# Attention and a gated feed-forward block in one kernel: output groups split in halves of 192 columns, single steps paired, value halves moved behind output steps

## The chip, the cores and the metric

The kernel runs on one core of a Trainium2 chip. A core has five engines with a queue each: TensorE (PE) for matrix products, VectorE (DVE) and ScalarE (ACT) for elementwise work, GpSimd (POOL), and SyncE (SP), which issues transfers. TensorE writes to PSUM, eight banks of 512 float32 columns by 128 partitions; everything else lies in SBUF. An engine works off its instructions in the order in which they were written; between engines, semaphores hold an instruction back until what it reads is there, or until the buffer that it overwrites has been read. The metric is the device time of one execution in microseconds.

## The reference

Eight batches of twelve heads, 448 positions, 64 columns a head; then a feed-forward block over 3584 tokens of 768 columns, with 1536 hidden columns. All inputs are float32, and the kernel loads them as float16.

```python
scores = np.matmul(q, k.transpose(0, 1, 3, 2)) / np.sqrt(64)
attn = np.exp(scores - np.max(scores, -1, keepdims=True))
attn = attn / (np.sum(attn, -1, keepdims=True) + 1e-09)
x = np.matmul(attn, v).transpose(0, 2, 1, 3).reshape(3584, 768)
g = x @ w_gate
out = (g / (1 + np.exp(-g)) * (x @ w_val)) @ w_out
```

## The kernel before

**Attention.** Heads go in 48 pairs. `qk` makes the scores of one chunk of keys for the two heads of a pair, transposed (keys on partitions, 2 x 448 queries in columns), in a tile `s` of two banks; ACT takes the exponential into `E` (L366 for the later pairs). `pv` multiplies `E` with the values, to which a column of ones is attached, into two accumulators `acc` (one bank each); DVE divides by the sums (L480, L481) into `xt`, and a transposing DMA on SP's queue puts that into `X`, with the 768 columns on partitions and tokens in columns. POOL's queue loads q, k and v and POOL copies q and k (L238) for the next pairs.

**Feed-forward, first half.** Tokens go in blocks of 384 and 512 columns. A `Step` makes one block of 128 hidden columns: a gate product `gp` (six matmuls, L586), ACT's tanh `sg` (L613), DVE's `t` = (sg + 1) gp (L639), a value product `vp`, and DVE's `hts` = t vp (L645). A block has twelve steps. `run_pair` runs two steps interleaved: the gate of one, the gate of two, the value of one, then the value of two *split* in halves of columns. The first half goes into a bank that step one left free (`spare`, shown as gp in the rows of the value weights), the second into a bank of its own (vp). `run_single` runs one step alone, split in the same way; `run_fv` runs one whole.

**Feed-forward, second half.** `OutPair.wide` makes the output of two chunks of 128 tokens, called a *group* below, with seven products in place of eight, from sums that DVE makes beforehand (`h_sums`, L569 to L572; the sums of the weights stay in SBUF). Each product is six matmuls of 128 x 384 (`OH` = 384), and they share three banks, a, c (both in tile `og`) and b (tile `ob`):

| product | bank | then |
|---|---|---|
| P1 | a | ACT copies it to p1 (L765) |
| P2 | c | DVE makes p15 from it and p1 (L767) |
| P3 | b | DVE writes p15 and b back to c (L760) |
| P4 | a, added to P1 | ACT copies it to the output (L772) |
| P5 | b, over P3 | DVE makes an output quarter of b and p15 (L760) |
| P6 | c, added to what DVE wrote | ACT copies it to the output (L783) |
| P7 | b, added to P5 | DVE makes the last quarter with p1 (L760) |

So P4 can't start before the copy to p1 has read a, and neither P5 nor P7 before DVE has read b. A third chunk of a block of 384 is done plainly, in four *output steps* of 12 matmuls of 192 columns (`plain_out`, L679), which ACT copies out (L686). Outputs collect in `osb` (four buffers) and are stored through SP's queue (L669).

**Order.** Pairs of heads and feed-forward are interleaved by hand in *visits*, one for each entry of a list. A visit issues, in this order: the scores of three chunks with their exponentials, the accumulations `pv` of one pair of heads, and then feed-forward work. One visit in seven has no accumulations; it is called bare. From the visit `base` on, which is visit 0 here, the list `VISITS` says what the work is: `(begins, nf, ng, no, ns)`, where nf counts steps (2 is a pair, 1 a single), ng groups, no output steps, and ns extra sums. If the next visit is bare, steps run one after the other and whole. The queues of ACT and DVE get their instructions in the same order, so that a group's ACT copies stand behind the three exponentials of its visit. Tiles `s`, `gp` of a step, `og` and `op` of an output step share three buffers of two banks (`ps_s`); `acc`, `vp` and `ob` share two buffers of one bank (`ps_f`).

The visits that differ, with the time at which their scores start in the profile before:

| visit | starts | before | after |
|---|---|---|---|
| 11 | 189.05 | group | half group |
| 12 | 197.51 | output step | pair, last half put off |
| 13 | 200.30 | pair | output step, put-off half |
| 14 | 207.23 | output step | output step, half group |
| 15 | 209.89 | pair | pair, last half put off |
| 16 | 216.99 | output step | output step, put-off half |
| 17 (bare) | 219.61 | pair | pair, last half put off |
| 18 | 225.82 | output step | output step, put-off half |
| 22 | 246.62 | group | half group |
| 23 | 255.08 | single (whole) | two whole steps |
| 25 | 263.50 | single | half group |
| 26 | 267.27 | group | pair |
| 27 | 276.12 | single | half group |
| 29 | 285.79 | single | half group |

Visits 19 to 21, 24 and 28 are pairs, 30 and 31 output steps, in both kernels; visits 0 to 10 are the same. After visit 31 come the last blocks, in `Unit`s (products with seven matmul chains of their own, L855) and groups, which the change leaves alone; POOL makes weight sums for them (L818 to L821) from visit 26 on.

Of the kernel before, what the change touches and what calls it, by code (L numbers as in the profile page):

```python
# [10 lines left out]
FP32 = mybir.dt.float32  # L11
FP16 = mybir.dt.float16
AF = mybir.ActivationFunctionType
# [3 lines left out]
HS = 4096.0  # L17
# [48 lines left out]
def kernel(  # L66
# [10 lines left out]
    nc = tc.nc  # L77
# [636 lines left out]
    class OutPair:  # L714
# [26 lines left out]
        def stored(self, z, lo=0, w=DM, queues=(nc.sync,)):  # L741
            store(self.osb[z], self.kk, self.c0 + (2 * self.t + z) * 128, 128, lo, w, queues, self.last)

        def wide(self, keep, add_sum, ns=(1, 2, 1)):
            osb = self.open()
            g = ps_s.tile([128, 2, 512], FP32, tag="s", name="og")
            a, c = g[:, 0, 0:OH], g[:, 1, 0:OH]
            if self.last:
                bs = ps_s.tile([128, 2, 512], FP32, tag="s", name="ob")
                parts = [(i * QW, QW, bs[:, i, 0:QW]) for i in range(2)]  # L750
            else:
                parts = [(0, OH, ps_f.tile([128, 512], FP32, tag="f", name="ob")[:, 0:OH])]
            p1, p15 = (k[:, 0:OH] for k in keep)
            both = (nc.sync, nc.scalar)

            def products(lhs, m, first=False):
                return [(lo, w, b, product(b, lhs, self.tt(m, lo, w), first)) for lo, w, b in parts]

            def combine(dst, x, scale, y, lo, w):
                return nc.vector.scalar_tensor_tensor(  # L760
                    dst[:, ds(lo, w)], x[:, ds(lo, w)] if scale == HS else x, scale, y, ALU.mult, ALU.add
                )

            product(a, self.hh(0, self.x), self.bb(0, 0, 0, OH), True)
            keep1 = nc.scalar.activation(p1, a, AF.Copy, scale=1.0 / HS)  # L765
            apart(product(c, self.hh(0, self.y), self.tt(0, 0, OH), True), keep1)
            done = [nc.vector.scalar_tensor_tensor(p15, c, 1.0 / HS, p1, ALU.mult, ALU.add)]  # L767
# [3 lines left out]
            apart(product(a, self.hh(1, self.x), self.bb(0, 1, 0, OH)), *done)  # L771
            left = nc.scalar.activation(osb[0][:, 0:OH], a, AF.Copy, scale=1.0 / HS)  # L772
            for one in done[1:]:
                tc.declare_no_dep(left.ins, one.ins, reason="another bank")
            if self.last:
                self.stored(0, 0, OH, both)
            for lo, w, b, mms in products(self.hs(1), 2):
                combine(osb[1][:, OH:], b, 1.0 / HS, p15[:, ds(lo, w)], lo, w)
            if self.last:
                self.stored(1, OH, OH, both)  # L780
            add_sum(ns[1])
            apart(product(c, self.hs(2), self.bb(1, 1, 0, OH)), left)
            nc.scalar.activation(osb[0][:, OH:], c, AF.Copy, scale=1.0 / HS)  # L783
            if self.last:
                self.stored(0, OH, OH, both)
            else:
                self.stored(0)
            ends = []
            for lo, w, b in parts:
                mms = product(b, self.hh(1, self.y), self.tt(3, lo, w))  # L790
                apart(mms, *ends)
                ends.append(combine(osb[1], b, 1.0 / HS, p1[:, ds(lo, w)], lo, w))
                if self.last:
                    self.stored(1, lo, w, both)
            if not self.last:
                self.stored(1)
            add_sum(ns[2])

# [145 lines left out]
    with tc.manual_schedule():  # L944
# [50 lines left out]
        def add_block(i, visits):  # L995
            if i < B - NB - 1:
                f1, own, n = block(i)
                fvq.extend(f1)
                kk, c0, hts = own
            else:  # L1000
                own = None
            t_out = NFB * OH / 2400.0
            if i == 0:
                oq.extend([(ffn2_steps(*own, by_half(range(n // 128), OH)), t_out)] * (2 * (n // 128)))
            if i < 2:
                if i:
# [12 lines left out]
            for pair in new:  # L1019
                pair.todo = pair.sums()  # L1020
                sums.extend(pair.todo)

        FIRST_STEPS = [2, 2, 1, 2, 1, 1, 1]
        VISITS = [
# [7 lines left out]
        ]  # L1032

# [36 lines left out]
                add_sum()  # L1070
            return 2 * step.time

        def run_pair():
            one, two = fvq.pop(0), fvq.pop(0)
            two.split, two.alone = True, gate_small[0]
            one.gate()
# [17 lines left out]
            step.finish()  # L1094
            add_sum()

        def run_steps(n):
            for _ in range(n - 2):
                run_fv()
            if n > 1:  # L1100
                run_pair()
            elif n:
                run_single()

# [105 lines left out]
        for x, (chunks, todo) in enumerate(plan):  # L1210
# [70 lines left out]
            else:  # L1281
# [177 lines left out]
```

## Time and profile before

| | |
|---|---|
| median of 3 runs | 426.39 us (426.32 to 426.64) |
| the profiled execution | 426.09 us, of which 424.3 us from first to last instruction |
| granted TensorE clock | 0.999 |
| TensorE | 4382 matmuls |
| visits 11 to 31 | 189.05 to 297.70 us |
| visit 11 (group) | 8.46 us, ACT busy 3.90, DVE 3.43 |
| visit 12 (output step) | 2.79 us, ACT busy 2.36, DVE 1.94 |
| visit 25 (single) | 3.77 us, ACT busy 2.98, DVE 2.35 |

A row of the timeline gives the start in us, the length, the engine (PEld is TensorE's weight load, which runs beside its matmuls), the line of the kernel, the operation, the tile written and those read, the shape, and how many instructions the row merges; in brackets stands how long the engine was idle before it, and for whom it waited. Matmuls overlap: one is shown some 170 ns longer than the next one's start allows, so the distance of starts is what a matmul costs.

### The profile page before, as it was taken

The page shows a single profiled execution, that of the slowest core. Times are in us where ns is not written, and L with a number is a line of the kernel's source. Part 1 is how long each engine was busy: PE and PEld are TensorE (multiplying, and loading weights), DVE is VectorE, ACT ScalarE, POOL GpSimd, SP SyncE. Part 2 cuts the span into 40 slices and gives each one's busy share as a digit, 9 for nine tenths or more (in the row PEclk, how much of TensorE's full clock was granted, in tenths as well). Part 3 has the DMA queues.
Part 4 walks back from the last instruction along what each step waited for, and adds up shares of the span by engine and source line. Part 5 has one row for each costly group of instructions (what it writes and reads, how often), then busy time and mean ns, then how long its engine had stood idle before and what let it go on. Part 6 is the DMA issues. An engine that isn't in the chain of part 4 may idle for free.

```text
span 424.3 us, 11026 instructions
## 1 busy us (share of the span) xinstructions
PE 417.6 (98%) x4382; PEld 263.7 (62%) x4382; DVE 265.2 (63%) x606; ACT 243.5 (57%) x385; POOL 229.6 (54%) x351
## 2 busy tenths in 40 slices
PE   8999999999999999999999999999999999999996
PEld 3666666655556676656656766667888655555554
DVE  4766562787669564674645765487776665565563
ACT  6976667646755654655666547569655125555221
POOL 8656625988886738349376772885999000000000
PEclk9999999999999999999999999999999999999999
DMA  9999999999999799969999999942100240000125
GB/s 137 181 201 200 200 173 192 139 159 207 135 153 152 118 147 138 170 93 177 120 130 131 133 137 149 103 115 43 22 2 19 96 122 28 2 0 2 37 76 150
DMA packets 107764, 49.73 MB, mean 117 GB/s; under 512 B 59840, under 2 KB 104512, under 8 KB 107712
## 3 DMA queue, kind: packets, MB, share of 16 engines
q0 software_dynamic: 46800, 24.56, 52.1%
q1 hardware_dynamic: 60640, 24.22, 32.6%
q8 instruction: 34, 0.56, 0.6%
q14 instruction: 18, 0.15, 0.2%
q10 hardware_dynamic: 272, 0.25, 0.2%
HBM read 49.55 MB, written 11.01 MB: 143 GB/s over the span
## 4 chain that ended last, share of the span: by engine, by line
PE 93%; ACT 3%; DVE 2%; DMA 1%; issue 1%; SPq 0%; DVEq 0%; ACTq 0%
PE gp L586 18%; PE vp L586 12%; PE un L855 10%; PE og L703 10%; PE acc L438 8%; PE ub L855 8%; PE ob L703 8%; PE s L346 5%; PE op L679 4%; PE acc L402 2%; PE s L376 2%; ACT E L384 1%; PE s L358 1%; ACT E L366 1%; PE tp L317 1%; PE op L1049 1%
## 5 line engine op out<-in xcount | busy, mean ns | idle before, releaser
L366 ACT ACTIVATE E<-s 128x896 f16<-128x896 f32 x126 | 106.6, 919 | 50.3 <-PE s L346 35.1
L238 POOL COPY qk<-qkraw 128x512 f16<-128x512 f16 x70 | 42.8, 655 | 57.3 <-DMA qkT<-qk 56.0
L586 PE MATMUL gp<-X,wg 128*128 128x384 f16 (+1 forms) x360 | 73.1, 348 | 0.0
L586 PE MATMUL vp<-X,wv 128*128 128x384 f16 (+3 forms) x360 | 64.2, 314 | 0.1
L639 DVE SCALAR_TENSOR_TENSOR t<-sg,gp 128x384 f32<-128x384 f32 (+1 forms) x60 | 36.1, 608 | 41.4 <-ACT sg L613 41.1
L586 PEld LDWEIGHTS <-wv 128*128 128x128 f16 x492 | 46.1, 98 | 24.5 <-issue 0.4
L178 POOL DMA_DIRECT2D vraw<-in_v_dram x72 | 44.1, 638 | 13.1 <-DVE hts L645 8.8
L586 PEld LDWEIGHTS <-wg 128*128 128x128 f16 x360 | 32.7, 98 | 27.2 <-issue 2.2
L178 POOL DMA_DIRECT2D qkraw<-in_k_dram x70 | 42.6, 627 | 5.8 <-DMA wo<-in_moe_w_out_dram 3.7
L384 ACT ACTIVATE E<-s 112x896 f16<-112x896 f32 x48 | 40.6, 917 | 8.0 <-PE s L376 8.0
L438 PEld LDWEIGHTS <-E 128*128 128x128 f16 (+2 forms) x1224 | 38.2, 98 | 9.2 <-issue 3.2
L613 ACT ACTIVATE sg<-gp 128x384 f32<-128x384 f32 (+1 forms) x60 | 32.0, 538 | 19.3 <-PE gp L586 16.6
L438 PE MATMUL acc<-vo,E 128*128 128x65 f16 (+2 forms) x1224 | 42.4, 193 | 0.1
L703 PEld LDWEIGHTS <-hts 128*128 128x128 f16 x270 | 25.9, 98 | 15.9
L645 DVE SCALAR_TENSOR_TENSOR hts<-t,vp 128x384 f16<-128x384 f32 (+3 forms) x60 | 31.4, 523 | 5.6 <-PE vp L586 2.1
L481 DVE TENSOR_TENSOR xt<-acc,R 128x256 f16<-128x256 f32 x72 | 30.6, 425 | 2.5
L201 POOL DMA_DIRECT2D qkraw<-in_q_dram x43 | 29.4, 685 | 4.2 <-DMA vraw<-in_v_dram 1.5
L346 PE MATMUL s<-qkT 64*64 64x448 f16 (+1 forms) x288 | 29.2, 353 | 0.5 <-DVE hts L645 0.2
L703 PE MATMUL og<-wo,hts 128*128 128x384 f16 x132 | 25.1, 326 | 0.0
L480 DVE RECIPROCAL R<-acc 128x4 f32<-128x4 f32 x72 | 12.7, 177 | 17.7 <-PE acc L438 17.5
L219 DVE COPY vo<-vraw 128x512 f16<-128x512 f16 (+1 forms) x48 | 19.7, 413 | 3.4 <-DMA vraw<-in_v_dram 3.4
L679 PE MATMUL op<-wo,hts 128*128 128x192 f16 (+1 forms) x168 | 21.4, 281 | 0.0
(185 smaller groups left out, 684.3 us busy)
## 6 DMA issues: line engine op xcount, KB each, us to landing
vraw<-in_v_dram POOLq DMA_DIRECT2D x72, 64.0 KB, 5.0
qkraw<-in_q_dram POOLq DMA_DIRECT2D x39, 112.0 KB, 4.4
qkraw<-in_k_dram POOLq DMA_DIRECT2D x68, 64.0 KB, 4.9
wg<-in_moe_w_gate_dram POOLq DMA_DIRECT2D x8, 288.0 KB, 9.8
wv<-in_moe_w_val_dram POOLq DMA_DIRECT2D x8, 288.0 KB, 10.5
wo<-in_moe_w_out_dram POOLq DMA_DIRECT2D x2, 1152.0 KB, 18.7
out_dram<-osb SPq DMA_DIRECT2D x7, 288.0 KB, 4.3
out_dram<-osb SPq DMA_DIRECT2D x6, 336.0 KB, 4.2
```

The costliest lines, as they stand in the source:

```text
L178: eng.dma_start(dst[ts(s, 64)], rows)
L238: nc.gpsimd.tensor_copy(dst.rearrange("p c h d -> p h c d"), src)
L346: nc.tensor.matmul(s[ts(half, m), hx, 0:S], lhsT=t[ts(hx, 64), ds((c + low(pr, hx)) * 128 + half * m, m)], rhs=t[ts(hx, 64), ds(NC * 128, S)],
L366: nc.scalar.activation(e[:, 0 : 2 * S].rearrange("p (h q) -> p h q", h=2), s[:, :, 0:S], AF.Exp, scale=sm_scale)
L384: nc.scalar.activation(e[:, :, 0:S], s[0:P, :, 0:S], AF.Exp, scale=sm_scale)
L438: nc.tensor.matmul(acc[ds(lo, m), ts(j, D + 1)], lhsT=e[rows, ds(hx * S + j * 128 + lo, m)], rhs=Vts[pr % NV][rows, hx, col, 0 : D + 1], s ...
L586: nc.tensor.matmul(dst[:, 0:w], lhsT=wslice(kind, self.fb, cb), rhs=X[kk][:, cb, ds(c0 + lo, w)], start=(cb == 0), stop=(cb == NCB - 1),)
L613: self.readers = [nc.scalar.activation(self.sg[:, 0:n], gp[:, 0:n], AF.Tanh, scale=0.5)]
L639: nc.vector.scalar_tensor_tensor(self.t1[:, 0:n], self.sg[:, 0:n], 1.0, self.gp[:, 0:n], ALU.add, ALU.mult)
L679: nc.tensor.matmul(op[:, 0:w], lhsT=hts[:, fb, ts(ch, 128)], rhs=wo[oh][:, fb, ds(off, w)], start=fb == 0, stop=fb == NFB - 1,)
L703: nc.tensor.matmul(dst, lhsT=lhs(n), rhs=rhs(n), start=first and n == 0, stop=n == NH - 1, skip_group_check=True)
L855: mm = nc.tensor.matmul(dst, lhsT=lhs[:, n], rhs=rhs[:, n], start=first and n == 0, stop=n == NK - 1, skip_group_check=True,)
```

## The change

`wide` takes a first column `m0` and a width `n`. With n = 192 it makes the seven products for columns m0 to m0 + 191 of both halves of the output; two calls make a group, the second one stores it. The groups of visits 2 and 6 stay whole; the three later ones are made in six halves, in visits of their own. `run_group` first runs the visit's output steps, if it has any. The single steps become members of pairs or, before the bare visit 24, whole steps. A pair that is followed by a visit with nothing but an output step leaves its last value half, six matmuls of 256 columns and DVE's product, for the end of that visit.

```diff
-        def wide(self, keep, add_sum, ns=(1, 2, 1)):
+        def wide(self, keep, add_sum, ns=(1, 2, 1), m0=0, n=OH):
...
-            a, c = g[:, 0, 0:OH], g[:, 1, 0:OH]
+            a, c = g[:, 0, 0:n], g[:, 1, 0:n]
+            at, whole = [ds(oh * OH + m0, n) for oh in range(2)], m0 + n == OH
...
-            product(a, self.hh(0, self.x), self.bb(0, 0, 0, OH), True)
+            product(a, self.hh(0, self.x), self.bb(0, 0, m0, n), True)
...
-            else:
+            elif whole:
                 self.stored(0)
...
-            (0, 2, 0, 0, 1), (0, 0, 1, 0, 0), (0, 0, 0, 1, 0), (0, 2, 0, 0, 0), (0, 0, 0, 1, 0),
+            (0, 2, 0, 0, 1), (0, 0, 1, 0, 0), (0, 2, 0, 0, 0), (0, 0, 0, 1, 0), (0, 0, 1, 1, 0),
             (0, 2, 0, 0, 0), (0, 0, 0, 1, 0), (0, 2, 0, 0, 0), (0, 0, 0, 1, 0), (0, 2, 0, 0, 0),
-            (4, 2, 0, 0, 1), (0, 2, 0, 0, 1), (0, 0, 1, 0, 0), (0, 1, 0, 0, 0), (0, 2, 0, 0, 0),
-            (0, 1, 0, 0, 0), (0, 0, 1, 0, 0), (0, 1, 0, 0, 0), (0, 2, 0, 0, 0), (0, 1, 0, 0, 0),
+            (4, 2, 0, 0, 1), (0, 2, 0, 0, 1), (0, 0, 1, 0, 0), (0, 2, 0, 0, 0), (0, 2, 0, 0, 0),
+            (0, 0, 1, 0, 0), (0, 2, 0, 0, 0), (0, 0, 1, 0, 0), (0, 2, 0, 0, 0), (0, 0, 1, 0, 0),
...
+        put_off = []
+
-        def run_pair():
+        def run_pair(later=False):
...
             two.value(0)
-            two.finish()
+            if later:
+                put_off.append(two.finish)
+            else:
+                two.finish()
...
-        def run_group():
-            pair = groups.pop(0)
+        def run_group(n):
+            pair = groups[0]
...
-            pair.wide(keep, add_sum, (1, 1, 0))
+            pair.wide(keep, add_sum, (1, 1, 0) if n == OH else (0, 1, 0), pair.begun, n)
+            pair.begun += n
+            if pair.begun == OH:
+                groups.pop(0)
...
-                for _ in range(ng):
-                    run_group()
+                if ng:
+                    for _ in range(no):
+                        run_o()
+                    run_group(ng * QW)
+                    no = 0
...
-                    run_steps(nf)
+                    run_steps(nf, nf == 2 and VISITS[x + 1 - base][1:4] == (0, 0, 1))
...
+                while put_off and not nf:
+                    put_off.pop(0)()
```

In `VISITS` the first two groups' ng becomes 2 (two quarters of 192, a whole group), so that ng now counts units of 192 columns.

More of the change, by code (lines that the diff above doesn't have):

```diff
@@ L751, in wide @@
             else:
-                parts = [(0, OH, ps_f.tile([128, 512], FP32, tag="f", name="ob")[:, 0:OH])]
-            p1, p15 = (k[:, 0:OH] for k in keep)
+                parts = [(0, n, ps_f.tile([128, 512], FP32, tag="f", name="ob")[:, 0:n])]
+            p1, p15 = (k[:, 0:n] for k in keep)
             both = (nc.sync, nc.scalar)
             def products(lhs, m, first=False):
-                return [(lo, w, b, product(b, lhs, self.tt(m, lo, w), first)) for lo, w, b in parts]
+                return [(lo, w, b, product(b, lhs, self.tt(m, m0 + lo, w), first)) for lo, w, b in parts]
             def combine(dst, x, scale, y, lo, w):
@@ L770, in wide @@
             add_sum(ns[0])
-            apart(product(a, self.hh(1, self.x), self.bb(0, 1, 0, OH)), *done)
-            left = nc.scalar.activation(osb[0][:, 0:OH], a, AF.Copy, scale=1.0 / HS)
+            apart(product(a, self.hh(1, self.x), self.bb(0, 1, m0, n)), *done)
+            left = nc.scalar.activation(osb[0][:, at[0]], a, AF.Copy, scale=1.0 / HS)
             for one in done[1:]:
@@ L777, in wide @@
             for lo, w, b, mms in products(self.hs(1), 2):
-                combine(osb[1][:, OH:], b, 1.0 / HS, p15[:, ds(lo, w)], lo, w)
+                combine(osb[1][:, at[1]], b, 1.0 / HS, p15[:, ds(lo, w)], lo, w)
             if self.last:
@@ L789, in wide @@
             for lo, w, b in parts:
-                mms = product(b, self.hh(1, self.y), self.tt(3, lo, w))
+                mms = product(b, self.hh(1, self.y), self.tt(3, m0 + lo, w))
                 apart(mms, *ends)
[L792 to L795, printed above, removed]
+                ends.append(combine(osb[1][:, at[0]], b, 1.0 / HS, p1[:, ds(lo, w)], lo, w))
+            if self.last:
+                self.stored(1, 0, OH, both)
+            elif whole:
                 self.stored(1)
@@ L1019, in add_block @@
             for pair in new:
-                pair.todo = pair.sums()
+                pair.todo, pair.begun = pair.sums(), 0
                 sums.extend(pair.todo)
@@ L1095, in run_single, with run_steps @@
             add_sum()
-        def run_steps(n):
+        def run_steps(n, later=False):
             for _ in range(n - 2):
@@ L1100, in run_steps @@
             if n > 1:
-                run_pair()
+                run_pair(later)
             elif n:
```

6 lines of the change are left out of this document (3 added, 3 removed), and 4 rows, old and new, of the table VISITS.

## The prediction

> Visits are numbered as the table above numbers them, and the seven products of a group P1 to P7 as they are issued.
>
> **What bounds the kernel now.** First the page: the share of busy time, and the chain that ended last.
>
> ```profile
> PE 417.6 (98%) x4382; PEld 263.7 (62%) x4382; DVE 265.2 (63%) x606; ACT 243.5 (57%) x385; POOL 229.6 (54%) x351
> PEclk9999999999999999999999999999999999999999
> PE 93%; ACT 3%; DVE 2%; DMA 1%; issue 1%; SPq 0%; DVEq 0%; ACTq 0%
> ```
>
> TensorE is the bound from end to end at the full granted clock, so an edit is worth what it changes on TensorE: the matmuls in its stream, and the holes between them. The stream's pitch is the same everywhere: the chain merges twelve 384-column matmuls to 1.95 us (162.5 ns each) and twelve 192-column ones to 0.99 us (82.5 ns). Both are columns / 2.4 plus 2.5 ns, with a weight load (98 ns) hidden under each. Half the columns therefore cost half the time plus 2.5 ns.
>
> Second, the holes, from the timeline of visit 11, a whole group. (The length of a PE row is modelled and runs past the next row's start; starts are what to read.)
>
> ```profile
> 189.05 0.74 PE L346 MATMUL s<-qkT 64*128 64x448 f16 x6
> 189.45 2.54 ACT L366 ACTIVATE E<-s 128x896 f16<-128x896 f32 x3 [2.31 <-PE s L346]
> 190.59 1.14 PE L703 MATMUL og<-wo,hts 128*128 128x384 f16 x6
> 191.86 0.51 ACT L765 ACTIVATE p<-og 128x384 f32<-128x384 f32 x1
> 192.81 0.56 DVE L767 SCALAR_TENSOR_TENSOR p<-og,p 128x384 f32<-128x384 f32 x1 [1.20 <-PE og L703]
> 193.51 1.14 PE L703 MATMUL og<-wo,hts 128*128 128x384 f16 x6
> 193.72 0.56 DVE L760 SCALAR_TENSOR_TENSOR og<-p,ob 128x384 f32<-128x384 f32 x1 [0.35 <-PE ob L703]
> 194.49 1.14 PE L703 MATMUL ob<-E,hsum 128*128 128x384 f16 x6
> ```
>
> The group starts at 190.59, while the three exponentials still occupy ACT to 191.99. The copy of P1 stands behind them and starts 1.27 us into the group. P4 (193.51) adds to the bank that this copy reads, P5 (194.49) overwrites the bank that the DVE combination of 193.72 reads. Both reads end before their matmul is due (192.37; 194.28): the whole group has no hole, because a product lasts 0.975 us.
>
> Third, the visits with little TensorE work: the timeline around the output step of visit 14, then the scores that follow the single steps of visits 25, 27 and 29.
>
> ```profile
> 206.03 0.69 DVE L645 SCALAR_TENSOR_TENSOR hts<-t,vp 128x512 f16<-128x512 f32 x1
> 206.49 0.82 PE L586 MATMUL vp<-X,wv 128*128 128x256 f16 x6
> 206.69 0.42 DVE L645 SCALAR_TENSOR_TENSOR hts<-t,gp 128x256 f16<-128x256 f32 x1
> 207.45 0.55 PE L346 MATMUL s<-qkT 64*64 64x448 f16 x8
> 208.81 1.15 PE L679 MATMUL op<-wo,hts 128*128 128x192 f16 x12
> 209.89 1.01 PE L346 MATMUL s<-qkT 64*128 64x448 f16 x6
> ...
> 267.49 0.85 PE L346 MATMUL s<-qkT 64*64 64x448 f16 x8
> ...
> 280.06 0.85 PE L346 MATMUL s<-qkT 64*64 64x448 f16 x8
> ...
> 289.39 0.55 PE L346 MATMUL s<-qkT 64*128 64x448 f16 x4
> 290.14 0.37 PE L346 MATMUL s<-qkT 64*128 64x448 f16 x2 [0.20 <-DVE hts L645]
> ```
>
> The score matmuls after such a visit take longer than in an ordinary one: 1.01 against 0.74 us after the output step of visit 14 (a bank waits for the exponential), 0.85 against 0.55 after the singles of visits 25 and 27, and 290.14 instead of 289.78 after the one of visit 29 (a bank waits for the last DVE product of the single). These holes are what the change can win.
>
> **The change part by part.** (1) *Holes removed.* After output steps: visit 13 0.10 (0.85 against 0.74), visit 15 0.25, visit 17 0.21 (0.15 before its second scores, 0.06 within them and behind them), visit 19 0.18. With 0.66 us of value product behind the output step, these visits last longer than three exponentials. After singles, which are gone: visits 26 and 28 0.27 each, visit 30 0.38, of which I give back 0.10 since the output step of visit 30 then comes earlier and visit 31 waits for its exponentials. After a whole group the second accumulator waits for the last 0.56 us combination: 0.09, 0.11, 0.11 in visits 12, 23, 27; with 192 columns (0.36 us) it no longer does. Sum: 0.74 + 0.82 + 0.30 = **-1.86 us**.
>
> (2) *Matmuls.* Three groups of 42 become six halves of 42, +126; four single steps (12 + 3 x 18 matmuls) become two whole steps and a pair (24 + 30), -12. 114 x 2.5 ns = **+0.29 us**.
>
> (3) *The half group's own chain.* A product is now 0.495 us. What it must cover is as long as before in its fixed parts. Durations at 192 columns: ACT copy 0.35 (output copy, L686, behind an exponential), DVE combination 0.36 (L760 at 192 columns in the last group: 0.361, 0.364); a DVE operation starts 0.03 after its releaser, a matmul 0.05; an evacuation starts 0.20 after the last matmul of its product gives way. From the start of the half: copy 1.27 to 1.62; P4 at 1.67 instead of 1.485 (hole 0.19); first DVE operation 1.66 to 2.01, combination 2.05 to 2.41; P5 at 2.455, where P4 ended at 2.17 (hole 0.285); P5 to 2.95, its combination 3.15 to 3.505; P6 to 3.445; P7 at 3.555 (hole 0.11). Together 0.58 us each in visits 11, 22, 27 and 29. Visit 25 follows a bare visit and its scores wait 0.11 themselves, so its exponentials end earlier against the group (copy at 1.10): 0.40. In visit 14 an output step (0.99) goes first, so the exponentials and that step's own copy are done 0.7 us into the group; the copy of P1 ends at 1.03, and only the two waits for DVE remain: 0.22. Sum 4 x 0.58 + 0.40 + 0.22 = **+2.94 us**. Bounds: nothing, as in the whole groups; or 0.9 each (5.4) if a DVE sum (0.55, L571) stands between the links.
>
> (4) *Value halves put off* (visits 12, 15, 17). The pair then ends with the half that goes into the first step's spare bank. Its DVE product can't start before the whole value's product ends (206.72), so it ends at 207.11 whatever TensorE does, while TensorE arrives 0.66 us sooner: the third scores of the next visit, due at 206.97, get that bank at 207.16. 0.19 us x 3 = **+0.57 us**. Below nothing is excluded, since the matmuls stay the same; above, the bound is 0.66 each. DVE's copy of v queues behind the put-off product, but it is for two visits later.
>
> (5) *Visit 23* is followed by a bare visit and so runs two whole steps; three h sums (0.55 each) stand on DVE among their four products. The second step's t then ends near 4.57 us after the visit's accumulations, its bank is wanted at 4.40 by the third scores: **+0.22 us** (0 to 0.5).
>
> (6) *At nothing:* SP's stores of two groups go out one to three visits later; SP is not the bound, four output buffers are used in the same rotation, and a store lands in about 4.3 us, far from its buffer's next use (over 20 us). POOL's loads, copies and weight sums keep their places among the visits; the sums are needed only after visit 31, which moves with them. If that cover went, POOL's 0.91 us pieces would show as holes in the units; today these are 0.08 at most.
>
> Sum: 2.94 + 0.57 + 0.22 + 0.29 - 1.86 = +2.16 us. The profiled execution took 426.09 us (span 424.3 and 1.8 around), so **428.2 us**; the median of the runs shown is 0.3 above that execution, within the spread that I leave.
>
> On the price of a narrow matmul the row says 82.5 ns at 192 columns. The Trainium skill, "TensorE: Matmul & The Clock Gate", section "Back-to-back issue gap", says that in a stream of weight loads and matmuls both set the spacing, and gives about 81 ns at 128 and 131 ns at 512 columns. An estimate between its two figures is 89 ns at 192 and 114 ns at 384, so that 252 narrow instead of 126 wide matmuls would cost 8.1 us more instead of 0.3, and the sum would be 436.0. The trace has 216 ns at 512 and 162.5 at 384 columns, so the row is used.
>
> **The rivals.** *The halves' chain is covered.* If the three waits in (3) were met in time, the change would save 1.86 and cost 1.08: 425.3 us, faster. It decides once a half waits less than 0.14 us on average (0.78 us over six). For it speaks that no whole group has a hole. Against it, the last group of all: there the first product into ob is followed by a P4 of 0.975 us and P5 still came 38 ns late, behind a 0.36 combination (417.12 to 417.17); halves have half that cover.
>
> *ACT is further ahead.* If the copy of P1 came as early in all halves as in visit 14, six halves would wait 0.22 each: 1.32 instead of 2.94, 426.6 us, no change. Against it: the exponentials start 0.40 us after a visit's first scores in every ordinary visit, and the group 1.54 after them.
>
> *DVE stands in the way.* A sum or a copy of v between the links adds 0.3 us a half: 430.0 us. For it: DVE's token sum took 1.26 us once beside POOL's sums (281.09). Against it: in program order these stand behind the chain.
>
> *The clock drops.* Waits inside a group could let the clock gate close. The granted clock was 0.999 with holes of 0.2 to 0.4 us in the rows above. At half rate six halves alone would need 3.4 us more each, 449 us. The Trainium skill's same page, section "A second HAM failure mode: psum-queue depth-cycling", tells of a kernel whose small idles between matmul groups did this; no run here shows it.
>
> **How the numbers follow.** Forecast 0.72 (427.4 to 429.2: visits 25 and 23 and the put-off waits each at their bounds). Covered 0.09, ACT ahead 0.09, DVE in the way 0.08, clock or spacing 0.02. The range reaches from the second rival, 426.4, to the third, 429.8; what lies outside is the first, the last and half of the third, 0.15. About 0.2% (0.85 us) is what a measurement tells from no change: faster 0.09, within 0.10, slower 0.81.
>
> **What would show it.** In the profile after: inside a half group P4, P5 and P7 start 0.19, 0.28 and 0.11 us after TensorE is free; ACT's copy (L766) starts 1.27 us into the half; after visits 12, 15 and 17 the scores' row grows by 0.19; the rows of 1.01 and 0.85 us are gone. The prediction is wrong if the halves show products 0.495 us apart with no hole, or if the score rows stay long.

## The result, and the profile after

The changed kernel takes 429.47 us (median of 6 runs, 429.09 to 429.71), the kernel before 426.46 on the same chip (6 runs, 426.29 to 427.11). The ratio is 1.0067, with a 95% interval of 1.0057 to 1.0077: 2.4 to 3.3 us slower. The forecast of 428.2 said slower by 2.2; the time lies inside its range of 426.4 to 429.8, but 1.3 us above the number itself and 0.3 above the inner band of 427.4 to 429.2. The profiled execution of the changed kernel took 429.71 us, with a span of 427.8.

The page of the changed kernel, its busy times, its clock and its chain:

```profile
PE 419.3 (98%) x4496; PEld 271.6 (63%) x4496; DVE 264.4 (62%) x616; ACT 245.3 (57%) x394; POOL 230.3 (54%) x351
PEclk9999999999999999999999999999999999999999
PE 90%; DVE 3%; DMA 2%; POOL 2%; ACT 2%; issue 1%; DVEq 0%; ACTq 0%; POOLq 0%
```

TensorE has the 114 matmuls more that the diff gives it (4496 for 4382), still at the full clock, and is on the chain for 90% of the span instead of 93%. Most of that difference isn't the loss: the shares of POOL and DMA lie in the first 20 us, where the chain runs through the loading of q, k and v, with 3.9 us of TensorE instead of 11.0. Within the visits, from 11 to 31, it goes through DVE for 6.3 us instead of 2.8, which points to waits. They are found by following TensorE through the visits. The timeline of visit 11, the first half group:

```profile
191.72 0.66 PE L703 MATMUL og<-wo,hts 128*128 128x192 f16 x6
192.71 0.66 PE L703 MATMUL ob<-E,hsum 128*128 128x192 f16 x6
193.00 0.35 ACT L766 ACTIVATE p<-og 128x192 f32<-128x192 f32 x1
193.38 0.36 DVE L768 SCALAR_TENSOR_TENSOR p<-og,p 128x192 f32<-128x192 f32 x1 [0.63 <-PE ob L703]
193.40 0.66 PE L703 MATMUL og<-wo,hts 128*128 128x192 f16 x6
193.84 0.36 DVE L761 SCALAR_TENSOR_TENSOR og<-p,ob 128x192 f32<-128x192 f32 x1
194.26 0.66 PE L703 MATMUL ob<-E,hsum 128*128 128x192 f16 x6 [0.20 <-DVE og L761]
194.75 0.66 PE L703 MATMUL og<-wo,hsum 128*128 128x192 f16 x6
194.95 0.36 DVE L761 SCALAR_TENSOR_TENSOR osb<-ob,p 128x192 f32<-128x192 f32 x1 [0.74 <-PE ob L703]
195.36 0.66 PE L703 MATMUL ob<-qkraw,hts 128*128 128x192 f16 x6
```

A product lasts 0.495 us, so P4 was due at 192.71 + 0.495 = 193.205 and starts at 193.40, when the copy of P1 (193.00 to 193.35) has read its bank: 0.19 late. P5 was due at 193.895 and comes at 194.26, behind the combination of 193.84: 0.37 late. P7, due at 195.245, comes at 195.36: 0.12 late. (The table of the products above says that P5 goes over P3; in the code it adds to b, like P7. The wait for DVE's reading of b is the same.) Visits 22, 25, 27 and 29 show the same three holes, 0.67 us each when the starts are taken to the nanosecond; in visit 14, behind an output step, P5 waits 0.16 and P7 0.12, 0.27 together. (These waits are counted by starts, against a pitch of 0.495; the idle time in a row's brackets is shorter, because a matmul's shown end lies some 0.17 us late.)

The put-off half, from the timeline at the end of visit 12 and the scores of visit 13:

```profile
201.59 0.69 DVE L645 SCALAR_TENSOR_TENSOR hts<-t,vp 128x512 f16<-128x512 f32 x1
202.14 0.94 PE L346 MATMUL s<-qkT 64*128 64x448 f16 x6
202.25 0.42 DVE L645 SCALAR_TENSOR_TENSOR hts<-t,gp 128x256 f16<-128x256 f32 x1
```

Six undisturbed score matmuls take 0.74 us; these take 0.94, since the last two want the bank that the product of 202.25 is reading until 202.67. It is so after visits 15 and 17 too: 0.188, 0.185 and 0.189 us by the starts of the matmuls.

What was won: the same pair stands in visit 28 in both orders, behind a single step before and behind a half group after. First its scores and accumulations before, then after:

```profile
280.06 0.85 PE L346 MATMUL s<-qkT 64*64 64x448 f16 x8
280.74 1.20 PE L438 MATMUL acc<-vo,E 64*64 64x65 f16 x40
```

```profile
282.00 0.55 PE L346 MATMUL s<-qkT 64*64 64x448 f16 x8
282.38 1.13 PE L438 MATMUL acc<-vo,E 64*64 64x65 f16 x40
```

The row of 0.85 is gone, and the row behind it is shorter as well: the visit went from 5.94 to 5.57 us, 0.37, where the prediction listed a hole of 0.27.

From the start of visit 11 to the first matmul of the units the kernel before took 108.65 us and the changed one 110.88: **+2.23 us, against a forecast of +2.16.** From there to the last matmul both take 122.3 us. Behind the last matmul's start, the nine profiles that have the changed `wide` (this one and those below) take 4.38 to 4.45 us and the five without it 4.16 to 4.31: about 0.15 us that the forecast didn't have. The change does touch the last group, in one place: its last two stores of 192 columns become one of 384. But the last store lands 3.04 to 3.08 us after the last matmul's start in both (two profiles of each), so the difference lies behind that landing, and its cause is open. And visit 11 itself starts at 190.19 instead of 189.05, although the instructions up to there are the same. This further 1.14 us is taken up with the last two runs below.

### The profile page after: what moved, and what is told of

Read it like the earlier page. It is cut to its first block, busy times and chain, and to the rows that moved or that the text cites. A ratio compares the mean times of both kernels' runs of the same rounds, so it can differ in the third digit from the quotient of the medians.

```text
span 427.8 us, 11280 instructions
## 1 busy us (share of the span) xinstructions
PE 419.3 (98%) x4496; PEld 271.6 (63%) x4496; DVE 264.4 (62%) x616; ACT 245.3 (57%) x394; POOL 230.3 (54%) x351
## 4 chain that ended last, share of the span: by engine, by line
PE 90%; DVE 3%; DMA 2%; POOL 2%; ACT 2%; issue 1%; DVEq 0%; ACTq 0%; POOLq 0%
PE gp L586 17%; PE vp L586 12%; PE un L856 10%; PE og L703 9%; PE ob L703 8%; PE acc L438 8%; PE ub L856 8%; PE s L346 5%; PE op L679 5%; PE acc L402 2%; DMA qkraw<-in_k_dram 2%; PE s L376 2%; PE s L358 1%; POOL qkraw L201 1%; PE tp L317 1%
## 5 line engine op out<-in xcount | busy, mean ns | idle before, releaser
L586 PE MATMUL vp<-X,wv 128*128 128x384 f16 (+3 forms) x360 | 65.1, 317 | 0.3
L586 PEld LDWEIGHTS <-wv 128*128 128x128 f16 x480 | 45.1, 98 | 25.4 <-DVE xt L481 0.5
L703 PEld LDWEIGHTS <-hts 128*128 128x128 f16 x342 | 31.1, 98 | 13.2 <-issue 0.9
L703 PE MATMUL og<-wo,hts 128*128 128x384 f16 (+1 forms) x168 | 26.1, 291 | 0.1
L703 PEld LDWEIGHTS <-hsum 128*128 128x128 f16 x204 | 18.5, 98 | 7.6 <-issue 1.1
L703 PE MATMUL ob<-E,hsum 128*128 128x192 f16 (+1 forms) x150 | 21.4, 281 | 0.6 <-DVE og L761 0.6
```

The lines of the kernel that those rows point to most:

```text
L586: nc.tensor.matmul(dst[:, 0:w], lhsT=wslice(kind, self.fb, cb), rhs=X[kk][:, cb, ds(c0 + lo, w)], start=(cb == 0), stop=(cb == NCB - 1),)
L703: nc.tensor.matmul(dst, lhsT=lhs(n), rhs=rhs(n), start=first and n == 0, stop=n == NH - 1, skip_group_check=True)
```

## The experiments

The theory is that of the prediction: each half pays its own chain of copy and combinations, and that is the loss. Rivals: the put-off halves or the rest of the new order lose the time; narrow products cost TensorE by themselves; the loss lies ahead of visit 11. In each of the comparisons "before" is the kernel before on the same chip, in the same series, so its median changes from one to the next.

**The exponential of the third scores moved behind the copy of P1**, in visits that hold nothing but a half group.

```diff
+                half_only = x >= base and VISITS[x - base][1:4] == (0, 1, 0)
-                qk(pr, c, small)
+                qk(pr, c, small, half_only and n == len(ordered) - 1)
...
             keep1 = nc.scalar.activation(p1, a, AF.Copy, scale=1.0 / HS)
+            while held:
+                held.pop(0)()
```

> The kernel after, with one edit: in the five visits that hold only a half group, the third exponential is given to ACT behind the copy of P1 instead of ahead of it. My theory (the holes in a half begin with a copy that stands behind the exponentials): P4 starts without a hole, P5 waits 0.12 to 0.16 us as in visit 14, P7 0.12 as before; a half loses 0.28 instead of 0.68 us, five halves 2.0 us less: about 427.5 us. Rival (DVE's chain is the bound, whatever ACT does): only the 0.19 us before P4 goes and reappears before P5; less than 0.5 us in all, 429.0 or more. A second rival: the later exponential makes the scores of the next visit wait, and nothing is gained.

Measured: 427.74 us (7 runs; before 426.35), ratio 1.0034 (1.0022 to 1.0046). Timeline of its visit 11:

```profile
191.09 0.33 ACT L775 ACTIVATE p<-og 128x192 f32<-128x192 f32 x1
191.32 0.91 ACT L370 ACTIVATE E<-s 128x896 f16<-128x896 f32 x1
191.38 0.66 PE L712 MATMUL ob<-E,hsum 128*128 128x192 f16 x6
191.88 0.66 PE L712 MATMUL og<-wo,hts 128*128 128x192 f16 x6
192.53 0.66 PE L712 MATMUL ob<-E,hsum 128*128 128x192 f16 x6
```

The copy starts 0.69 us into the half (190.40) in place of 1.28; P4 follows P3 after 0.495 with no hole, P5 comes 0.16 late. Four of the five visits went from 5.76 to 5.37. So the hole of P4, and 0.21 of that of P5, come from ACT's queue: the exponentials stand ahead of the copy. The fifth, visit 22, went the other way, to 6.00 us:

```profile
247.38 1.44 POOL L238 COPY qk<-qkraw 128x512 f16<-128x512 f16 x2 [0.93 <-DMA qkT<-qk]
```

```profile
247.65 0.70 DVE L219 COPY vo<-vraw 128x512 f16<-128x512 f16 x1
248.27 0.95 DVE L581 TENSOR_TENSOR hsum<-hts,hsum 128x768 f16<-128x768 f16 x1
```

```profile
249.84 0.67 PE L712 MATMUL ob<-E,hsum 128*128 128x192 f16 x6 [0.34 <-DVE xt L490]
```

These are POOL, DVE and TensorE in turn. While POOL copies, DVE's copy of v takes 0.70 us (0.29 undisturbed) and its sum 0.95 (0.55); the accumulators are read late, and P3, which needs the bank of one of them, waits 0.51. This is the rival "DVE stands in the way". The edit doesn't bring it about by itself: in the second and third profiles of the changed kernel, shown below, P3 of visit 22 waits 0.32 and 0.18, and in the run with both mends not at all. Visits 11 to 31 took 109.63 us in this profile, 1.25 less than in the changed kernel. Behind them 0.28 us was lost again in the units, where one ACT copy starts 0.27 later behind its product than in the changed kernel; the same is seen in the run with both mends, the edit touches nothing there, and the cause is open.

**The first half of a put-off value in a bank of its own.**

```diff
-            two.split, two.alone = True, gate_small[0]
+            two.split, two.alone, two.own = True, gate_small[0], later
...
-                dst = ps_f.tile([128, 512], FP32, tag="f", name="vp") if half else self.spare
+                own = half or self.own
+                dst = ps_f.tile([128, 512], FP32, tag="f", name="vp") if own else self.spare
```

> The kernel after, with one edit: in the three pairs whose last value half is put off, the first half goes into a bank of its own (vp's pool) and not into the first step's spare bank. My theory (the third scores of the next visit wait for the DVE product that reads the spare bank): the holes of 0.19 us in front of the third scores of visits 13, 16 and 18 vanish, 0.56 us less: about 428.9 us. Rival: the wait moves to the second accumulator, which now shares that bank, and the time stays at 429.5.

Measured: 428.78 us (4 runs; before 426.35), ratio 1.0062 (1.0047 to 1.0077). Visits 13, 16 and 18 take 3.27 us instead of 3.48; visits 11 to 31 take 110.26, 0.61 less. The scores of visit 13 are back at their ordinary length:

```profile
202.12 0.74 PE L346 MATMUL s<-qkT 64*128 64x448 f16 x6
```

**No put-off**, the rest as changed.

```diff
-                    run_steps(nf, nf == 2 and VISITS[x + 1 - base][1:4] == (0, 0, 1))
+                    run_steps(nf)
```

> The kernel after without the put-off: pairs end with both value halves, and the three visits with an output step alone are as short as before. My theory: the three holes of 0.19 us go, and the holes behind the output steps of visits 13, 16 and 18 come back (in the profile before 0.26, 0.21 and 0.18 us for such visits): no change within 0.3 us, 429.2 to 429.8. Rival: the put-off is a cost alone, 428.9 or less. Rival: it pays as meant, 430.0 or more.

Measured: 429.96 us (4 runs), ratio 1.0089 (1.0067 to 1.0111). Visits 12 to 19 take 41.47 us with no put-off and 41.39 with it: the old holes behind the output steps come back (0.16, 0.22 and 0.16 before the second scores of visits 14, 17 and 19), the put-off's three of 0.19 go. The put-off is worth nothing either way; the loss isn't there. (The median is 0.16 above what was expected. Visit 24 took 5.24 us in this profile, and in the first of the changed kernel 4.96; the table below shows that it varies.)

**One group alone halved**, in the order of before: visit 11 a half, visit 12 its output step and the other half.

```diff
-            (0, 2, 0, 0, 1), (0, 0, 1, 0, 0), (0, 0, 0, 1, 0), (0, 2, 0, 0, 0), (0, 0, 0, 1, 0),
+            (0, 2, 0, 0, 1), (0, 0, 1, 0, 0), (0, 0, 1, 1, 0), (0, 2, 0, 0, 0), (0, 0, 0, 1, 0),
```

(with `wide` and `run_group` as changed, whole groups as ng = 2, and no put-off)

> The kernel before, with one group alone made in halves: that of visit 11, whose second half goes into visit 12 behind its output step. No pair is made of singles and nothing is put off. If a half pays its own chain, visit 11 gets the holes that the changed kernel has there (0.19, 0.37 and 0.12 us, 0.68 together), visit 12 those of its visit 14 (0.16 and 0.12, 0.28), the 42 extra matmuls cost 0.10, and the wait of the second accumulator behind the group (0.09) and that behind the output step of visit 12 (up to 0.10) go: visits 11 and 12 together 0.8 us longer, and the time 0.6 to 1.0 us above the kernel before. If the halves were free and the loss of the changed kernel came from the rest of its new order, the two visits would be 0.1 us shorter to 0.1 us longer and the time would be that of the kernel before, within 0.2%.

Measured: 427.53 us (10 runs; before 426.79 in 30), ratio 1.0015 (1.0002 to 1.0027). Visits 11 and 12 took 5.76 + 6.38 = 12.14 us instead of 8.46 + 2.79 = 11.25, 0.89 more, and visits 11 to 31 together 0.72 more. The timeline of the second half, in visit 12:

```profile
197.36 0.66 PE L703 MATMUL og<-wo,hts 128*128 128x192 f16 x6
198.84 0.66 PE L703 MATMUL og<-wo,hts 128*128 128x192 f16 x6
199.50 0.66 PE L703 MATMUL ob<-E,hsum 128*128 128x192 f16 x6
199.99 0.66 PE L703 MATMUL og<-wo,hsum 128*128 128x192 f16 x6
200.60 0.66 PE L703 MATMUL ob<-qkraw,hts 128*128 128x192 f16 x6
```

P4 comes on time, 1.48 after P1, since the output step gave ACT a lead; P5 comes 0.66 after P4 and P7 0.61 after P6, where 0.495 is the pitch. A halved group thus costs its holes here as in the changed order, one cheap half (0.27) and one dear one (0.67).

**The put-off alone**, on the kernel before, and then **the put-off with its own bank**, on the kernel before. The edits are those above.

> The kernel before, with the put-off value halves alone: the pairs of visits 13, 15 and 17 leave their last half for the end of the output steps of visits 14, 16 and 18. By the prediction each put-off costs 0.19 us at the next visit's third scores, 0.56 together, and takes away the holes behind these three output steps (0.25, 0.21 and 0.18 as listed in the prediction, 0.64, and up to 0.1 each more that was hidden in stalled score matmuls): the three pairs and output steps together 0.1 to 0.4 us shorter, and the time within 0.2% of the kernel before, 0.1 to 0.4 us below it. If the put-off itself were the loss of the changed kernel, the time would be 1 us or more above the kernel before.

> As the kernel with the put-off alone, but the first half of the value goes into a bank of its own, so that the next scores do not wait for its product. If that wait is the whole price of a put-off, 0.19 us a time goes, 0.56 together: the holes of 0.19 before the third scores of visits 14, 16 and 18 are absent, and the time is 0.6 to 0.9 us below the kernel before, 425.5 to 425.8 where that has 426.4. If the bank only moves the wait (the accumulators use the same two banks), the time is that of the kernel with the put-off alone.

Measured: the put-off alone 426.63 us (12 runs), ratio 0.9994 (0.9984 to 1.0005), no change; visits 13 to 19 went from 35.20 to 35.11 us. With its own bank 425.31 us (6 runs; before 426.79), **ratio 0.9967 (0.9953 to 0.9981): faster than both kernels.** Visits 13 to 19 take 34.51 us, 0.69 less than before. The scores of visit 14, with the put-off alone and then with its own bank:

```profile
207.24 0.75 PE L346 MATMUL s<-qkT 64*64 64x448 f16 x8
```

```profile
206.51 0.55 PE L346 MATMUL s<-qkT 64*64 64x448 f16 x8
```

By the medians the gain is 1.5 us, more than expected; the visits account for 0.7 of it, and the interval begins at 0.8. In its profiled execution visit 11 also started 0.28 earlier, which varies from execution to execution by the runs below, so 0.7 is the safer figure for the edit.

**Both mends on the changed kernel.**

> The changed kernel with both mends at once: the exponential of the third scores behind the copy of P1 in visits with a half group alone, and the first value half of a put-off pair in a bank of its own. If the two losses lie in separate places, the gains measured for each alone add up: 1.7 and 0.7 us, the time 2.4 us below the changed kernel, 427.0, or 0.6 above the kernel before; by the visits, five halves 0.40 shorter and three put-offs 0.19 shorter, 2.56, it is 426.9. What is left above the kernel before is then the waits of P5 and P7 for DVE (0.28 in each of six halves, 1.7) less what the new order took away. If the two gains overlap, or the longer wait of visit 22 that came with the first mend comes again, 427.5 or more.

Measured: 426.94 us (12 runs; before 426.79), ratio 1.0007 (0.9997 to 1.0018). The two gains add up, and visit 22 takes 5.37 here. Visits 22 to 31 take 48.70 us and took 48.71 before: with the copy in time, halves and pairs are worth just what groups and singles were. (Visits 11 to 31 are 0.37 shorter than before; the 0.28 in the units and the 0.15 behind the last matmul take that back.) What is left is in every half the 0.16 of P5 and the 0.12 of P7.

**The halves' results unread.**

```diff
+            half = n != OH
+            free = self.hts[:, 0, 0:n]
+            ra, rc = (free, free) if half else (a, c)
...
-            keep1 = nc.scalar.activation(p1, a, AF.Copy, scale=1.0 / HS)
+            keep1 = nc.scalar.activation(p1, ra, AF.Copy, scale=1.0 / HS)
...
-                done.append(combine(c, p15, HS, b, lo, w))
+                done.append(combine(osb[1][:, at[0]] if half else c, p15, HS, free if half else b, lo, w))
```

(and the other five readings of a, b and c likewise; the outputs of these halves are not computed)

> The changed kernel, but in the six half groups the copies on ACT and the sums on DVE read a tile in SBUF in place of the three banks, and nothing is written back to the third bank. What it leaves out is the reading of the products, so these two groups of outputs (four chunks of tokens) are not computed; every instruction, its length and its place in the queues stay. If the whole loss of the changed kernel is the wait of P4, P5 and P7 for those reads, all holes inside halves go: 0.68 in each of five and 0.28 in visit 14, 3.7 us together, the visits with a half alone take 5.08 instead of 5.76, and the time is 425.8, below the kernel before by 0.6. If the narrow products cost TensorE time by themselves, the visits stay above 5.3 with products more than 0.50 us apart, and the time stays above 427. If the next wait takes over (the scores behind a shorter visit, for their exponentials), the holes inside halves go but half or more of it comes back between visits: 427.5.

Measured: 426.05 us (10 runs; before 426.62), ratio 0.9980 (0.9959 to 1.0002). Timeline of the same half group:

```profile
190.83 0.66 PE L703 MATMUL og<-wo,hts 128*128 128x192 f16 x6
192.32 0.66 PE L703 MATMUL og<-wo,hts 128*128 128x192 f16 x6
192.81 0.66 PE L703 MATMUL ob<-E,hsum 128*128 128x192 f16 x6
193.31 0.66 PE L703 MATMUL og<-wo,hsum 128*128 128x192 f16 x6
193.80 0.66 PE L703 MATMUL ob<-qkraw,hts 128*128 128x192 f16 x6
194.39 0.38 PE L358 MATMUL s<-qkT 64*64 64x448 f16 x4
```

Every product now comes 0.495 us after the one before it, and visits 11, 25, 27 and 29 take 5.09 or 5.10 us instead of 5.76 or 5.77. The loss of 2.9 us is gone: the holes inside the halves are enough to make up all of it, and the rest of the change, taken alone, is no loss. Visits 11 to 31 took 108.17 us, 2.71 less than in the changed kernel and 0.48 less than before. Of the 3.62 that the holes held, the rest was lost where DVE was slow again, as in the first experiment: P3 of visit 22 waits 0.51 behind a DVE copy of 0.70 and a sum of 0.95, and the third scores of visit 24 wait 0.58 instead of 0.22. The lengths did not all stay as expected: the combinations now read SBUF and took up to 0.65 us for 0.36, and ACT's later copies, which no longer wait for their products, ran up to 1.9 us earlier. Neither shows in the visits behind the halves, 12, 23, 26, 28 and 30, which are as long as in the changed kernel (within 0.02 us).

**Both kernels again**, unchanged: once the changed one, in the first series, and then both for the work ahead of visit 11.

> The kernel after once more, unchanged, for a second profile. In the first one visit 11 started 1.14 us later than in the profile before, though both kernels are the same instruction for instruction up to there; 0.8 of it is one stop of TensorE at 17 us, in the middle of matmuls that wait for no semaphore. If that belongs to the program (its instructions arrive later), visit 11 starts at 190.1 again, within 0.3 us; if it differs from execution to execution, it starts anywhere between 189.0 and 190.3. Visits 11 to 31 take 2.2 us longer than before in both cases.

> The kernel before once more, for the work ahead of visit 11 alone, which is the same program in both kernels. In the two profiles compared visit 11 starts at 189.05 before and at 190.19 after, and 188.86 to 190.26 in the other runs of the changed order. If that is chance from execution to execution, this run starts visit 11 anywhere from 188.8 to 190.3, and visits 11 to 31 take 108.65 again; if the place of later work in the program decided it, it starts at 189.05 within 0.1.

> The kernel before a third time, for its start of visit 11: so far 189.05 and 189.20, and 188.77 to 189.50 in the three other runs that keep its order. If the program up to there decides nothing, it starts between 188.8 and 190.3 like the changed kernel's; if only the changed order can be late, below 189.6 again.

> The changed kernel a third time, for its start of visit 11: so far 190.19 and 189.28, and 188.86 to 190.26 in the five other runs with its order, four of seven above 189.8. If chance decides, between 188.8 and 190.3 again, and visits 11 to 31 take 110.9 to 111.5. If its later code costs it something early, above 189.8 more often than not.

| | time, median (runs) | visit 11 starts | visits 11 to 31 | visit 24 |
|---|---|---|---|---|
| before, as shown | 426.46 (6) | 189.05 | 108.65 | 4.71 |
| before, second | 426.10 (1) | 189.20 | 108.65 | 4.74 |
| before, third | 426.27 (8) | 189.59 | 108.65 | 4.71 |
| after, as shown | 429.47 (6) | 190.19 | 110.88 | 4.96 |
| after, second | 429.93 (2) | 189.28 | 111.45 | 5.46 |
| after, third | 428.94 (4) | 188.98 | 111.18 | 5.25 |

The start of visit 11 varies from execution to execution in both orders; the changed kernel's third, at 188.98, is earlier than all three of the kernel before. The largest piece of the 1.14 us is one stop of TensorE near 17 us, between the second and third of three equal matmuls. First the changed kernel as shown, then the kernel before in its third profile:

```profile
17.28 0.28 PE L516 MATMUL acc<-ident,xt 128*128 128x128 f16 x2
18.34 0.22 PE L516 MATMUL acc<-ident,xt 128*128 128x128 f16 x1 [0.79 <-issue]
```

```profile
17.17 0.28 PE L516 MATMUL acc<-ident,xt 128*128 128x128 f16 x2
18.07 0.22 PE L516 MATMUL acc<-ident,xt 128*128 128x128 f16 x1 [0.63 <-issue]
```

The stop, with "issue" where a releaser would stand, is there in some executions of either kernel and absent in others. So the 1.14 us of the first pair of profiles is no fixed price of the change. That the change has no part in the start at all isn't shown: over all runs here visit 11 starts between 188.77 and 189.59 in the six profiles that keep the order of before, and between 188.86 and 190.26 in the eight with the changed order, four of them above 189.8, and the means lie 0.4 us apart. What is an effect of the change is the spread of visit 24, 4.96 to 5.46 us, where the kernel before has 4.71 to 4.74. In the second profile of the changed kernel DVE's h sums met POOL's copies:

```profile
257.85 0.77 DVE L571 TENSOR_TENSOR hsum<-hts 128x768 f16<-128x768 f16 x1
258.66 0.85 DVE L572 TENSOR_TENSOR qkraw<-hts,hsum 128x768 f16<-128x768 f16 x1
```

```profile
257.60 1.50 POOL L238 COPY qk<-qkraw 128x512 f16<-128x512 f16 x2 [5.42 <-DMA qkT<-qk]
```

```profile
260.02 0.38 PE L346 MATMUL s<-qkT 64*64 64x448 f16 x4 [0.56 <-DVE t L639]
```

0.77 and 0.85 in place of 0.55 and 0.56, and the third scores wait for the second step's t, which stands behind the sums on DVE: 0.73 us by the starts, 0.56 of it shown as idle. Over the three pairs of profiles visits 11 to 31 differ by 2.23, 2.80 and 2.53 us, on average 2.5, and with the 0.15 at the end 2.7, which lies in the interval of the measured loss (2.4 to 3.3).

## Why the prediction was right, and where its sum was off

The sign and the mechanism were right, and the size nearly: the change in the visits came out at +2.23 for a forecast of +2.16, in part by luck, since two of its terms were too small by about as much. The time alone would not have told the forecast from a rival, for 429.47 lies nearer to the 430.0 of "DVE stands in the way" than to 428.2; the profile decides. By its steps, from the first pair of profiles:

| step | forecast | measured |
|---|---|---|
| (1) holes removed | -1.86 | about -2.5, as what the other rows leave of +2.23, and read visit by visit |
| (2) matmuls | +0.29 | +0.29: 114 more, 82.5 ns at 192 columns |
| (3) the half group's own chain | +2.94 | +3.62 (5 x 0.67 + 0.27) |
| (4) put-off halves | +0.57 | +0.56 |
| (5) visit 23 and the bare visit behind it | +0.22 | +0.23; 0.5 to 0.7 in the other two profiles |
| (6) at nothing | 0 | 0 to the last matmul (122.3 us behind visit 31 in both), about +0.15 behind it |

**Step (3) was 0.68 too small.** P4 at 0.19 and P7 at 0.12 came as worked out. P5 was put at 0.285 and is 0.37: the two DVE operations in a row were spaced 0.04 us apart in the working, and lie 0.10 apart in the trace (193.74 to 193.84). That is 0.08 in each of five halves, and 0.05 in visit 14. The larger single miss is visit 25, put at 0.40 because its scores would wait and so give the exponentials a lead; in the new order that wait is gone, and the visit pays 0.67 like the others. Moving work ahead of visit 25 had changed the very row from which its discount was read. (The row of the exponentials, 189.45 to 191.99, and that of the copy behind them, from 191.86, overlap by 0.13; the 1.27 of the working goes by the copy's start and held.)

**Step (1) was about as much too small**, so that the sum came out right by the cancelling of two errors. A hole between two score matmuls isn't all that a late bank costs. The accumulations behind the scores were drawn out too (1.20 against 1.13 us in visit 28), and the visit gained 0.37 where 0.27 was listed. Visit 26 shows the same, by its group against that of visit 11 (8.85 to 8.46, of which 0.03 is the other shape of its scores, as in visits 21 and 20: 0.36 where 0.27 was listed), and visit 30 0.43 where 0.38 was. The 0.11 that visit 25 waited itself was named, but not counted as removed; with what it drew out behind it, it is 0.18. The visits behind whole groups and behind output steps gave some 0.1 more each, taken together, than was listed (the 0.30 for the groups is 0.31 by its own terms). The 0.10 given back in visit 31 came as 0.11. For the first stretch the listed holes held: the put-off alone gained 0.09 us net, by 0.57 paid and 0.64 removed.

**Step (4)** held to 0.01 us, and the run with its own bank shows that its cause is the one named: the bank, not the order. **Step (5)** lies at the upper bound and a little over it when POOL's copies fall on the h sums; the bound of 0.5 was drawn without them. Step (6) had no term for the end of the program.

**The rivals.** Their times in the prediction, 426.6 and 430.0 for the second and the third, lie 0.2 off the ends of the range that is said to reach to them. "The halves' chain is covered" falls with the holes, 0.60 us a half on average where its limit was 0.13 (0.78 over six, put at 0.14), and with the kernels that remove them. "ACT is further ahead" is refuted for visits with a half alone, where the copy starts 1.28 us in, and true where an output step goes first (0.27 in visit 14 of the changed kernel and in visit 12 of the single halved group). "DVE stands in the way" didn't happen within the halves of the first profile of the changed kernel, but did in visit 22 of its other two (P3 late by 0.32 and 0.18, which made the visit no more than 0.05 us longer, as the holes behind it shrank) and of two variants (0.51). The granted clock was 0.998 to 1.0 in every profile, so no run here shows the depth-cycling of which the Trainium skill's page "TensorE: Matmul & The Clock Gate" tells. Its spacing, by which 252 narrow matmuls would cost 8.1 us more, is refuted: unread halves run at 0.495 us a product, 82.5 ns a matmul.

Of the 1.3 us between forecast and median, 0.3 is the spread of visit 24 beyond its first value (2.5 against 2.23), 0.4 the distance of the profiled execution of before, on which the forecast was built, to the median beside the changed kernel's (426.09 to 426.46), and 0.15 the end of the program; the rest is within the scatter ahead of visit 11, and isn't resolved further.

## What to carry to other kernels

When each product needs an evacuation of the last but one, compare the length of a product with that of the evacuation and its fixed parts before making products shorter. In this kernel nothing showed at 0.975 us a product; at 0.495 each half paid 0.67 us, and where work (an output step) or a reordered queue (the copy ahead of the exponential) gave the first link a lead, it paid 0.27. When a stall is taken away, look at the rows behind it as well, and when a discount is read from a row, ask whether the change leaves that row as it is. A put-off that only moves a wait is worth nothing until the buffer behind the wait is separate: with the bank it was 0.7 us, without it none.

## What was not expected of the hardware

DVE's 16-bit operations from SBUF lengthened when they lay beside POOL's copies: a copy from 0.29 to 0.70 us, once to 1.01, a sum from 0.55 to 0.77, 0.85 and 0.95, and POOL's two copies beside them from 1.17 to between 1.44 and 1.82. The Trainium skill, "SBUF — State Buffer", section "Who interferes with whom", says that a DVE instruction with two SBUF inputs, or one in a two-port mode, and a POOL instruction that reads SBUF hold a shared pair of ports against each other. The direction agrees. The combinations that read PSUM, which make up the halves' chain, kept their 0.36 us. In the run with the halves unread they read both inputs from SBUF: one beside POOL's copies took 0.65 us, the two behind it 0.61 together.

TensorE stopped near 17 us in five of the fourteen profiles, of either kernel's order, with no semaphore as releaser; by the starts of its matmuls the stop took 0.25 to 0.95 us. A fetch of instructions (16 KB, 0.97 us) had landed shortly before, at 16.1 us before and 16.9 after, and over all profiles the two go together. In the five with the stop the fetch landed between 16.12 and 16.88, and the matmul behind the stop began 1.34 to 1.48 us after the landing. In eight it had landed by 16.09, and the same matmul came in its turn (0.03 late in one), never less than 1.4 us after the landing. In the last one, the run with no put-off, the fetch landed at 16.48, but TensorE itself was an us late, so that the matmul was due 1.9 us after it and came without a stop. That speaks for the fetch as the cause. No run moved the fetch alone, so it isn't shown.
